# Gelu and silu on two items at once, third-level key sums, earlier x tiles and held-back values in a planned attention + MLP kernel

## Chip, cores, metric

One core of one Trainium2 chip. The metric is device microseconds of a whole execution; smaller is better. ACT is the scalar engine, DVE the vector engine, PE the matmul engine (PEld its weight loads), POOL the GpSimd engine, SP the engine that issues transfers. Spans in a profile are 1.8 to 2.4 us shorter than the time that is reported for the run. "Granted clock" is the share of the full PE clock that the trace shows as granted.

## The reference, cut

```python
xn = layernorm(x)                       # x: 2048 x 1024, bf16
q, k, v = split(xn @ wqkv)              # 32 heads of 32
s = softmax(q k^T / sqrt(32)) v @ wo    # attention
h = gelu(layernorm(xn) @ w1 + b1)       # 3584 wide, tanh form
g = silu(h @ w2 + b2)
return x + s * g
```

## The kernel before

The kernel doesn't write its instruction order by hand. It records operations with estimated durations, runs a list scheduler over them on the host (the *planner*), and emits each engine's instructions in the order that came out. The order is then fixed: an engine that waits for one instruction can't take the next.

Eight groups of four heads give 512 *units* (256 queries x 256 keys x 4 heads). A unit is 8 score matmuls, two exponentials of 1024 columns on ACT, and 8 matmuls with V. Softmax denominators come from matmuls with a matrix of ones ("ones-quads", 4 column-tiled matmuls each). To need fewer of them, DVE first adds key blocks of the exponentials together. Between the units PE does the *dense* work: projections, w1, w2 and, near the end, the output projection wo.

```python
def commit(o, t):                                  # planner: a DMA
    ...
        state["bw"] = max(state["bw"], t) + o.nbytes / 210.0     # bytes per ns
        o.fin = state["bw"] + 1900.0
    ...
def unit(u, pv):                                   # scores, then exponentials
    o = add("PE", s_fn, 235.0, TL, ..., mode="r")  # row tiled
    for h in range(2):
        x = act(... ACT.Exp ..., c_act(1024), ..., 0)
    ...
def ones_pair(u, pv):                              # two units
    pa = dve(PA[a0:a0+2] = P[..,0,:] + P[..,1,:])  # first level, 2048 columns
    pb = dve(PA[a0] = PA[a0] + PA[a1])             # second level, 1024
    ...                                            # late ones are dropped; PE then does more quads
    if u < NOPA or ...: plan.skip.append(pa)       # NOPA = 24: none for the first 24 units
def w1_item(c, pi):                                # 256 x 256 of the hidden layer
    ... 16 matmuls in 8 chunks ...
    dve(xb = psum + b1); dve(sq = xb * xb); dve(ut = (sq + 1/GA) * xb)
    act(ut = tanh(GC * GA * ut))                   # 512 columns
    dve(h = (ut + 1) * xb)
```

The softmax here doesn't subtract the row's maximum and nothing guards it: scores larger than these inputs give would overflow.

## Time and profile before

| | before |
|---|---|
| time, runs of the first comparison | 1062.28 us median (1061.9 to 1063.47, 4 runs) |
| span of the profiled run | 1060.2 us |
| busy PE / DVE / ACT | 97% / 89% / 97% |
| first-level and second-level adds on DVE | 243 and 219 |
| ones-quads on PE | 319 |

The lines are in the prediction below. An ACT record lasts longer than the slot that its instruction takes: exponentials are 1243 ns long on average, but their median distance from start to start is 904 ns. I therefore measure *spacing*, from the start times in the trace, and cut every run in three:

- **start**: start of exponential 32 (counted from 0), by when the prologue is over;
- **middle**: from there to the start of the last exponential, number 1023;
- **tail**: from there to the end of the span.

Within the middle, *excess* is what exponentials are spaced above 904 ns, and a *gap* is a single one over 300 ns. The kernel before has start 63.97, middle 981.06, tail 15.19; 10.83 us of excess, but not one gap. (The recorded expectations below quote starts and tails from another zero; they differ by up to 0.5 us from the ones here, which count from the first instruction as `prof` does.)

### The profile page before, as it was taken

The page shows a single profiled execution, that of the slowest core. Times are in us where ns is not written, and L with a number is a line of the kernel's source. Part 1 is how long each engine was busy: PE and PEld are TensorE (multiplying, and loading weights), DVE is VectorE, ACT ScalarE, POOL GpSimd, SP SyncE. Part 2 cuts the span into 40 slices and gives each one's busy share as a digit, 9 for nine tenths or more (in the row PEclk, how much of TensorE's full clock was granted, in tenths as well). Part 3 has the DMA queues.
Part 4 walks back from the last instruction along what each step waited for, and adds up shares of the span by engine and source line. Part 5 has one row for each costly group of instructions (what it writes and reads, how often), then busy time and mean ns, then how long its engine had stood idle before and what let it go on. Part 6 is the DMA issues. An engine that isn't in the chain of part 4 may idle for free.

```text
span 1060.2 us, 32647 instructions
## 1 busy us (share of the span) xinstructions
PE 1026.5 (97%) x14502; PEld 643.7 (61%) x14562; DVE 946.9 (89%) x1585; ACT 1028.9 (97%) x1186; POOL 31.2 (3%) x42
## 2 busy tenths in 40 slices
PE   7999999999999999999999999999999999999998
PEld 5756466556665566566665566466665666665443
DVE  8479898999999998899989998999999998978996
ACT  4999999999999999999999999999999999999994
POOL 5500000000000000000000000000000000000000
PEclk9999999999999999999999999999999999999999
DMA  9335166522674466423763476224765776662442
GB/s 268 111 96 158 42 179 190 144 76 71 186 207 126 113 193 196 113 57 112 206 192 105 122 199 195 74 76 121 212 180 151 221 217 190 179 197 70 134 140 87
DMA packets 285798, 156.52 MB, mean 148 GB/s; under 512 B 23642, under 2 KB 276570, under 8 KB 285658
## 3 DMA queue, kind: packets, MB, share of 16 engines
q1 hardware_dynamic: 285658, 154.44, 51.0%
q8 instruction: 114, 1.87, 0.8%
q14 instruction: 26, 0.21, 0.1%
HBM read 142.35 MB, written 12.06 MB: 146 GB/s over the span
## 4 chain that ended last, share of the span: by engine, by line
ACT 93%; PE 4%; DVE 2%; DMA 1%; issue 0%; SPq 0%; POOL 0%; POOLq 0%
ACT P L1067 86%; ACT ut L939 5%; PE ps L668 3%; ACT gw L971 2%; DVE stats L823 1%; DMA hT<-in_A_x_dram 1%; PE ps L663 1%; ACT big L814 0%; PE ps L1058 0%; PE ps L803 0%; DVE yT L911 0%; POOL gw L847 0%; DVE V L740 0%; DVE mv L825 0%; SPq L693 0%
## 5 line engine op out<-in xcount | busy, mean ns | idle before, releaser
L1067 ACT ACTIVATE P<-ps 128x1024 bf16<-128x1024 f32 x1024 | 986.8, 1243 | 5.3 <-PE ps L1058 5.3
L1087 DVE TENSOR_TENSOR PA<-P 128x2048 bf16<-128x2048 bf16 x243 | 294.7, 1215 | 25.4 <-ACT P L1067 24.1
L668 PE MATMUL ps<-yT,w1r 128*128 128x256 bf16 x1792 | 234.9, 275 | 2.3 <-DVE xb L931 1.1
L668 PE MATMUL ps<-w2r,hT 128*128 128x256 bf16 x1792 | 226.9, 273 | 0.3 <-DVE nv L1121 0.2
L668 PEld LDWEIGHTS ps<-yT,w1r 128*128 128x128 bf16 x1792 | 162.1, 98 | 60.5 <-issue 28.6
L668 PEld LDWEIGHTS ps<-w2r,hT 128*128 128x128 bf16 x1792 | 162.2, 98 | 51.0 <-issue 30.5
L1091 DVE TENSOR_TENSOR PA<-PA 128x1024 bf16<-128x1024 bf16 x219 | 147.7, 684 | 1.4
L663 PE MATMUL ps<-P,V 128*32 128x256 bf16 x4096 | 142.8, 274 | 0.6 <-DVE xb L931 0.4
L668 PE MATMUL ps<-big,qk 128*128 128x512 bf16 (+2 forms) x522 | 120.9, 357 | 5.7 <-issue 2.1
L668 PE MATMUL ps<-qk,big 128*128 128x256 bf16 (+1 forms) x723 | 121.2, 305 | 2.5 <-issue 1.3
L663 PEld LDWEIGHTS ps<-P,V 128*32 128x32 bf16 x4096 | 97.7, 96 | 33.1 <-issue 19.6
L1058 PE MATMUL ps<-QKT 32*128 32x256 bf16 x2048 | 101.7, 273 | 7.4 <-ACT P L1067 5.9
L1058 PE MATMUL ps<-qk 32*128 32x256 bf16 x2048 | 101.9, 273 | 6.2 <-ACT P L1067 2.1
L939 ACT ACTIVATE ut<-ut 128x512 f32<-128x512 f32 x112 | 94.5, 855 | 0.0
L668 PEld LDWEIGHTS ps<-qk,big 128*128 128x128 bf16 x736 | 65.3, 98 | 41.5 <-issue 13.3
L931 DVE TENSOR_TENSOR xb<-ps,b1T 128x512 bf16<-128x512 f32 x112 | 76.6, 684 | 13.9 <-PE ps L668 12.6
L941 DVE SCALAR_TENSOR_TENSOR hT<-ut,xb 128x512 bf16<-128x512 f32 x112 | 76.4, 684 | 5.9 <-ACT ut L939 5.2
L668 PEld LDWEIGHTS ps<-big,qk 128*128 128x128 bf16 x568 | 47.7, 98 | 52.4 <-issue 15.6
L1058 PEld LDWEIGHTS ps<-QKT 32*128 32x128 bf16 x2048 | 30.3, 92 | 76.6 <-ACT P L1067 75.9
L937 DVE SCALAR_TENSOR_TENSOR ut<-sq,xb 128x512 f32<-128x512 bf16 x112 | 76.1, 682 | 0.3
L1058 PEld LDWEIGHTS ps<-qk 32*128 32x128 bf16 x2048 | 30.4, 92 | 71.6 <-ACT P L1067 67.4
L663 PE MATMUL ps<-PA,ones 128*32 128x256 bf16 x1068 | 56.0, 274 | 0.3 <-DVE PA L1091 0.3
(75 smaller groups left out, 532.2 us busy)
## 6 DMA issues: line engine op xcount, KB each, us to landing
w1r<-in_B_w_dram SPq DMA_DIRECT2D x112, 512.0 KB, 4.4
w2r<-in_B_w_dram SPq DMA_DIRECT2D x128, 448.0 KB, 4.4
qk<-in_A_wqkv_dram SPq DMA_DIRECT2D x16, 256.0 KB, 3.2
g_scratch<-gw SPq DMA_DIRECT2D x32, 128.0 KB, 3.0
o_scratch<-ot SPq DMA_DIRECT2D x56, 64.0 KB, 2.8
big<-o_scratch SPq DMA_DIRECT2D x28, 128.0 KB, 3.5
hT<-in_A_x_dram SPq DMA_DIRECT2D x10, 256.0 KB, 5.5
qk<-in_A_wqkv_dram SPq DMA_DIRECT2D x4, 512.0 KB, 4.4
```

The lines of the kernel that those rows point to most:

```text
L663: ins = e.matmul(dst(j), lhsT=lhsT(j), rhs=rhs(j), start=start, stop=stop, tile_position=(0, 32 * j), skip_group_check=True)
L668: return e.matmul(dst, lhsT=lhsT, rhs=rhs, start=start, stop=stop, skip_group_check=True)
L823: dve(lambda e, t=t, c=c: e.bn_stats(stats[:, t, c, :], xst[t][:, c * 512:(c + 1) * 512]), 600, [XS(t)], [("st", t, c)], 1)
L931: dve(lambda e: e.tensor_tensor(xb_t[i3][:].rearrange("p (k t) -> p k t", k=2), bank(it.bank).rearrange("p (k t) -> p k t", k=2), b1T[:, 2 ...
L937: dve(lambda e: e.scalar_tensor_tensor(ut_t[i3][:], sq_t[p % 2][:], 1.0 / GA, xb_t[i3][:], op0=ALU.add, op1=ALU.mult), c_f32(512), [("sq", ...
L939: act(lambda e: e.activation(ut_t[i3][:], ut_t[i3][:], ACT.Tanh, scale=GC * GA), c_act(512), [("ut", i3)], [("ut", i3)], 1)
L941: dve(lambda e: e.scalar_tensor_tensor(hT[:, hs].rearrange("p k t -> p (k t)"), ut_t[i3][:], 1.0, xb_t[i3][:], op0=ALU.add, op1=ALU.mult), ...
L971: act(lambda e: e.activation(zh_t[zi], z_t[zi], ACT.Tanh, scale=0.5), c_act(512), [("z", zi)], [("zh", zi)], 1)
L1058: ins = e.matmul(bank(b0[j], kk * 256, (kk + 1) * 256), lhsT=QKT[sl][32 * j:32 * j + 32, 1, kb * 128:(kb + 1) * 128], rhs=QKT[sl][32 * j:3 ...
L1067: x = act(lambda e, h=h: e.activation(P[pi][:, 2 * h:2 * h + 2].rearrange("p j k q -> p (j k q)"), ps[:, pr[h] * 1024:(pr[h] + 1) * 1024], ...
L1087: pa = dve(lambda e: e.tensor_tensor(PA_all[:, a0:a0 + 2].rearrange("p u j q -> p (u j) q"), P_all[:, p0:p0 + 2, :, 0, :].rearrange("p u j ...
L1091: pb = dve(lambda e: e.tensor_tensor(PA[a0][:], PA[a0][:], PA[a1][:], op=ALU.add), c_b16(1024), [("PA", a1)], [("PA", a0)], PBPRIO)
```

## The change

Its intent: fewer ACT instructions (one tanh for two items), less PE work (a third level of key sums; value matmuls placed after scores so that PE changes its tiling mode less), an earlier start. The diff, cut to its core:

```diff
-GRACE2 = 600 ; RESERVE = 300 ; NOPA = 24 ; OLAG = 1 ; GRACE1 = 8000
+GRACE2 = 1200; RESERVE = 800 ; NOPA = 0  ; OLAG = 0 ; GRACE1 = 2500
+GRACE3 = 600 ; FINE = 1 ; XF = 3 ; ADJ = 300 ; SPLIT = 2       (further dates changed)
@@ planner
-                state["bw"] = max(state["bw"], t) + o.nbytes / 210.0
+                state["bw"] = max(state["bw"], t) + o.nbytes / 280.0
@@ planner, opening a value item
+                        r = max(bf[0], it.chunks[0].ready, it.trigger.fin)
+                        if state["mode"] != "r" and state["dopen"] is not None:
+                            r = max(r, it.trigger.fin + ADJ)
@@ planner, prologue: work that is due may interrupt an open value item   (cut)
@@ DMA issue on SP
-            return add("SP", fn, 70, ...)
+            return add("SP", fn, 430, ...)
@@ x tiles
-        load_x(0)
-        load_x(1)
+        for t in range(XF):
+            load_x(t)
         wk0 = load_qk(0, 1)
         wq0 = load_qk(0, 0)
@@ w1_item (w2_item's silu likewise)
-            for k in range(8):                      # chunks of two matmuls
+            for k in range(16 // FINE):             # of one
+            if p % 2 == 0:
+                return it
+            dve(h = xb * xb)                        # 1024
+            dve(ut = (h + 1/GA) * xb)               # 1024
+            act(ut = tanh(...))                     # 1024
+            for r in halves: dve(h[r] = (ut[r] + 1) * xb[r])
@@ key sums, now for four units
+            add8 = dve(PA[a0] = PA[a0] + PA[a2])    # third level, 1024
```

Not shown: the planner's other estimates changed too, among them the q and k weight loads, counted at 1.5 times their bytes.

## The prediction

> **What bounds the kernel now.** I read the page first, then ACT's own waits, then the chain in order of time, then the groups by form, and last the two ends as timelines. The page's sums leave three candidates:
>
> ```profile
> PE 1026.5 (97%) x14502; PEld 643.7 (61%) x14562; DVE 946.9 (89%) x1585; ACT 1028.9 (97%) x1186; POOL 31.2 (3%) x42
> ...
> ACT 93%; PE 4%; DVE 2%; DMA 1%; issue 0%; SPq 0%; POOL 0%; POOLq 0%
> ```
>
> PE and ACT both show 97%, but the chain that ended last is 93% ACT. The waits decide it:
>
> ```profile
> PEld ps L1058 <- ACT P L1067: 143.3, 490, 1.3
> ...
> ACT big L814 <- PE ps L803: 11.2, 7, 6.0
> ...
> ACT P L1067 <- PE ps L1058: 5.3, 5, 3.0
> ```
>
> The score matmuls' weight loads (L1058) wait 143.3 us in all for the exponentials (L1067) to free a PSUM pair; ACT waits 16.5 us in the whole run (and 0.7 us at the very start). PE runs ahead of ACT, not behind. ACT's timeline shows where its idle time lies:
>
> ```profile
> 8.19 1.51 ACT L814 ACTIVATE big<-ps 128x1024 bf16<-128x1024 bf16 x2 [5.98 <-PE ps L803]
> 12.69 1.94 ACT L1067 ACTIVATE P<-ps 128x1024 bf16<-128x1024 f32 x2 [2.98 <-PE ps L1058]
> ...
> 20.67 1.94 ACT L814 ACTIVATE big<-ps 128x1024 bf16<-128x1024 bf16 x2 [2.46 <-PE ps L803]
> ...
> 61.63 1.94 ACT L1067 ACTIVATE P<-ps 128x1024 bf16<-128x1024 f32 x2 [0.92 <-PE ps L1058]
> ```
>
> The bracket is idle time before the row. After 61.6 us there is none until the last exponential ends at 1046.1 us (start 1039.47 plus 6.62): 984.46 us of wall time, 984.45 busy. So the time is startup idle 0.7 + 11.2 + 5.3 = 17.2 us, ACT work 1028.9, and a tail of 1060.2 - 1046.1 = 14.1. Sum 1060.2, the span; the timed median is 1.9 us longer.
>
> ACT's work by kind, from the merged chain:
>
> ```profile
> 110.53 26.56 ACT P L1067 x29
> 137.60 9.17 ACT P L1067 x10
> ...
> 621.12 1.01 ACT ut L939 x2
> ```
>
> 26.56 / 29 gives 0.916 us per exponential; the gap from 110.53 + 26.56 = 137.09 to 137.60 is one tanh of 512 columns, 0.51 us. (The group page's 1243 and 855 ns are start-to-end times which overlap; spacing is what counts.) Check: 1024 x 0.9165 + 144 x 0.513 (112 gelu, 32 silu) + 16 transposed copies (14.9) + 1.5 = 938.5 + 73.9 + 14.9 + 1.5 = 1028.8.
>
> **What the Trainium skill says.** "Perfetto Trace Analysis", Identifying the Most-Contended Engine, says matmul occupancy is no measure for TensorE and that occupancy serves for ScalarE. The trace agrees: PE's 97% hides 143 us of load waits, ACT's 97% is real. "VectorE: DVE Perf Modes", The TRN2 errata, says SBUF-source operations of VectorE and ScalarE pay a fixed cost once per instruction, so one larger tile pays it once. ACT agrees: an exponential takes 0.9165 for 1024 columns; if a column costs the page's 1.2 GHz cycle, 0.833 ns, the exponential leaves 0.063 us fixed and the 512-column tanh 0.513 - 0.427 = 0.086. "TensorEngine Tiling (Array Packing)", Key Properties, says that changing tiling mode drains TensorE; that is what putting values (column tiled) next to scores (row tiled) is to save. Here such a drain would lie in PE time that is not on the path.
>
> **The change part by part.**
>
> *Gelu and silu on pairs.* 144 tanh of 512 become 72 of 1024. A tanh of 1024 is estimated at 0.086 + 0.853 = 0.94 us. Saving 72 x (2 x 0.513 - 0.94) = 72 x 0.086 = 6.2 us of ACT, all on the path, since ACT has no idle time there. With the slope of the two PSUM copies instead ((1033 - 592) / 512 = 0.86 ns) it would be 5.2. I take 6.
>
> *DVE side of the pairs.* Square: 112 x 0.416 become 56 x 0.684 (the 1024-column bf16 add of L1091 is the same form), 8.3 us less. The add-and-multiply before tanh: 112 x 0.682 become 56 x 1.22 (0.684 = 0.153 fixed + 1.04 ns x 512, so 1.22 for 1024), 8 us less. Silu's last step, 2.4 us less. The product into hT stays in halves. Together 19 us less DVE, off the path.
>
> *Third-level sums.*
>
> ```profile
> L1087 DVE TENSOR_TENSOR PA<-P 128x2048 bf16<-128x2048 bf16 x243 | 294.7, 1215 | 25.4 <-ACT P L1067 24.1
> L1091 DVE TENSOR_TENSOR PA<-PA 128x1024 bf16<-128x1024 bf16 x219 | 147.7, 684 | 1.4
> L663 PE MATMUL ps<-PA,ones 128*32 128x256 bf16 x1068 | 56.0, 274 | 0.3 <-DVE PA L1091 0.3
> L663 PE MATMUL ps<-P,ones 128*32 128x256 bf16 x208 | 7.1, 273 | 0.0
> ```
>
> Before, 256 pairs of units need (1068 + 208) / 4 = 319 ones-quads. A third add of 0.684 us for each of 127 groups of four would be 87 us of DVE; no longer leaving out the first 24 units adds 12 x 1.215 + 12 x 0.684 = 23; the longer grace of the second level brings back at most the 23 adds dropped as late (256 - 12 - 2 - 219), 16 us. 946.9 + 87 + 23 + 16 - 19 = 1054, which is the whole span, so the planner must drop about half of the third adds as late. I expect 40 to 90 of them and DVE at 94 to 97%. PE then needs about 200 quads; 115 fewer at 0.11 us (spacing of the P,ones quads: 48 matmuls in 1.49 us at 51.4) are 13 us of PE. None of it is on the path but in the tail.
>
> *x tiles ahead of weights.*
>
> ```profile
> 2.72 5.91 DMA hT<-in_A_x_dram
> 8.65 1.29 DVE stats L823 x2
> 10.38 0.56 DVE stats L823
> ```
>
> The third x tile is issued at 2.72 behind the two weight slices and lands at 8.63; DVE has holes until then and is then busy without a break to 34.6, giving statistics for one pair of tiles every 3.5 us. With that tile third in the queue, its two statistics (1.3 us) move into the holes. The fourth tile has the same bytes ahead of it and gains nothing. So all of the key production moves up by about 1.3 us. The weights come later by some 256 KB at 281 GB/s, 0.9 us: with landings of 4.3 to 4.8 us after issues at 1.6 and 2.1 they arrive at about 7 to 8, still ahead of their first use at 9.27. Letting key work interrupt an open value item in the prologue, and planning DMA issue at its true 430 ns, may give another 1 us. The first 9 us of ACT idle (5.98 + 2.98) depend on tiles 0 and 1 and stay. Startup idle 17.2 becomes about 15.
>
> *Tail.* After the last exponential PE has 42 matmuls of 512 columns, 9.24 us in the chain. The last block's four output items need 4 x 8 = 32; the other 10 (2.2 us) are older work that was late. With 13 us of PE freed some of it gets done earlier; I take half, 1.1 us.
>
> *The rest* (new projection dates, single-matmul chunks, holding values back 300 ns, smaller buffers merged, statistics kept in the tanh buffer) moves PE and DVE work about within a loop that ACT bounds: 0, with some risk.
>
> Sum: 1028.9 - 6 = 1022.9 work; 15 + 13 idle; span 1051, time 1052.8. I say 1052.5.
>
> **The rivals.**
>
> *DVE becomes the bound.* For: 89% now, and up to 107 us of adds want in. The chain evacuation, square, add, tanh, product gets longer with pairs (two instructions of 1.2 us instead of 0.7 between PSUM and hT), and ACT runs in a fixed order, so a tanh or a score pair planned too early stalls it. Against: the adds that are late are dropped when planned, evacuations keep first priority, and ACT waits for DVE nowhere in the trace before. It would show as ACT waiting on the ut tile. Cost 5 to 25 us: 1058 to 1078.
>
> *PE was the true bound.* For: 97% busy. Then fewer ones-quads (13 us) and fewer mode drains count in full, and the time would go to 1035 or so. Against: PE's loads wait 143 us on ACT while ACT has no gap for 984 us; ACT's work alone plus the two ends cannot go below 1022.9 + 9 + 11 = 1043 span. I give it 2%.
>
> *The startup gain is hidden anyway.* POOL needs 0.70 + 0.19 + 2 x 1.2 = 3.3 us per pair of tiles against DVE's 3.5, so an earlier tile may only move the wait to POOL, and the weights may arrive late for 9.27. Then 1055.
>
> **Range and chances.** The pairs' 5 to 6 us are nearly sure; startup and tail 0 to 6 more; new waits up to 8 the other way. Range 1046.5 to 1059.5. Faster by 2% needs 1041, below the 1043 + 1.9 that ACT's work allows: 3%. Slower by 2% (above 1083) needs ACT idle of over 25 us in the middle: 3%.
>
> **What would show it.** Right: ACT work 1022 to 1024 us with 72 tanh of 1024 spaced about 0.94, no ACT idle between some 60 us and the last exponential, third tile landing before 7 us and the second pair of exponentials before 21.5 instead of 22.49, fewer than 250 ones-quads, DVE at 94 to 97%, tail 12 to 14 us. Wrong: ACT waits on DVE or on scores in the middle totalling over 3 us, exponentials spaced other than 0.9165, startup idle under 12 or over 18.

## The result, and the profile after

1064.17 us median (1062.75 to 1064.93, 4 runs) against 1062.28. Ratio 1.0014, 95% interval 0.9997 to 1.0032: the same. Ratios here are the mean time of one kernel's fast runs over that of the other's fast runs of the same rounds, so not quite the ratio of the medians quoted. The changed kernel was timed in this first comparison only. In the later rounds the kernel before took 1060.6 to 1060.8, so the difference of a variant to the changed kernel comes out 1 to 3 us lower by the times than by the ratios, which are used below.

The page of the changed kernel, engines and the chain that ended last:

```profile
PE 1025.0 (97%) x14334; PEld 637.7 (60%) x14334; DVE 972.6 (92%) x1506; ACT 1024.8 (97%) x1114; POOL 34.1 (3%) x42
...
PE 48%; ACT 43%; DMA 4%; DVE 3%; POOL 1%; issue 0%; POOLq 0%
```

The bound changed its face. The chain was 93% ACT; now PE has 48% of it and DMA 4%. The waits of the changed kernel (who, for whom, us in total, times, longest):

```profile
PEld ps L1125 <- ACT P L1134: 130.5, 450, 2.7
...
ACT big L860 <- PE ps L849: 11.2, 6, 6.3
ACT P L1134 <- PE ps L1125: 9.8, 11, 2.9
...
PE ps L714 <- DMA w1r<-in_B_w_dram: 4.4, 7, 1.1
```

ACT's wait for scores went from 5.3 to 9.8 us, and PE now waits for w1 weights, which it did not before. The groups by form (count, busy us, mean ns):

```profile
L1155 DVE TENSOR_TENSOR PA<-P 128x2048 bf16<-128x2048 bf16 x251 | 303.9, 1212 | 16.6 <-ACT P L1134 15.4 <-PE ps L714 0.5
...
L1160 DVE TENSOR_TENSOR PA<-PA 128x1024 bf16<-128x1024 bf16 x202 | 137.8, 689 | 1.7
...
L709 PE MATMUL ps<-PA,ones 128*32 128x256 bf16 x968 | 49.3, 276 | 0.1
...
L1163 DVE TENSOR_TENSOR PA<-PA 128x1024 bf16<-128x1024 bf16 x58 | 40.0, 690 | 1.3
...
L709 PE MATMUL ps<-P,ones 128*32 128x256 bf16 x80 | 2.9, 273 | 0.0
```

58 third-level adds survived; second-level ones fell by 17 (202, were 219). Ones-quads are (968 + 80) / 4 = 262, were 319.

Where the 1.3 us between the two profiled spans come from:

| us | before | after | difference |
|---|---|---|---|
| start | 63.97 | 63.10 | -0.9 |
| middle | 981.06 | 982.68 | +1.6 |
| - tanh in it | 74.37 | 68.22 | -6.2 |
| - excess of exponentials | 10.83 | 18.60 | +7.8 |
| tail | 15.19 | 15.78 | +0.6 |

So the pairs gave what they should, and the middle took it back, with 10 gaps over 300 ns that sum to 8.4 us. **The middle.** One gap, in the timeline of the changed kernel (start us, length us, engine, and in brackets the idle time before and its releaser):

```profile
199.24 2.55 SPq L936 DMA_DIRECT2D w1r<-in_B_w_dram  x2
...
204.66 0.38 PE L714 MATMUL ps<-yT,w1r 128*128 128x256 bf16 x2 [1.09 <-DMA w1r<-in_B_w_dram]
...
205.42 1.94 ACT L1134 ACTIVATE P<-ps 128x1024 bf16<-128x1024 f32 x2 [0.75 <-PE ps L1125]
```

Two w1 matmuls stand in PE's order in front of the next scores. Their weights are not there, PE waits 1.09 us, the scores come late, and ACT is idle for 0.75. The weights landed at 204.5, 5.29 us after the issue at 199.24.

By what PE had waited for just before them, the ten gaps divide so: seven (5.4 us of the 8.4) follow a wait for w1 weights, one (0.35) a wait for w2 weights, one (1.57, at 101.73) a stretch at half clock that is shown further down, and one (1.05, at 909.02) a wait for DVE, which had not yet emptied a PSUM bank:

```profile
907.27 1.36 PE L714 MATMUL ps<-yT,w1r 128*128 128x256 bf16 x11 [0.86 <-DVE xb L985]
...
909.02 1.94 ACT L1134 ACTIVATE P<-ps 128x1024 bf16<-128x1024 f32 x2 [0.65 <-PE ps L1125]
```

**The start.** The same view of the changed kernel, from 33.8 us:

```profile
33.84 1.21 DVE L1155 TENSOR_TENSOR PA<-P 128x2048 bf16<-128x2048 bf16 x1
33.88 1.73 POOL L888 TENSOR_TENSOR lnp<-lnp,mhalf 128x2 f32<-128x2 f32 x1
...
35.31 1.21 DVE L1155 TENSOR_TENSOR PA<-P 128x2048 bf16<-128x2048 bf16 x1
...
35.69 0.89 POOL L890 TENSOR_TENSOR lnp<-lnp 128x2 f32<-128x2 f32 x1
...
39.11 1.02 ACT L860 ACTIVATE big<-ps 128x1024 bf16<-128x1024 bf16 x1 [1.66 <-PE ps L849]
```

and the same two POOL operations in the kernel before:

```profile
34.68 0.70 POOL L842 TENSOR_TENSOR lnp<-lnp,mhalf 128x2 f32<-128x2 f32 x1
35.46 0.19 POOL L844 TENSOR_TENSOR lnp<-lnp 128x2 f32<-128x2 f32 x1
```

The exponentials were well ahead at first (number 8 started at 32.74, before at 37.18). Then DVE began key-sum adds, which the kernel before does not do for its first 24 units; POOL's power operation took 1.73 us instead of 0.70 and its small multiply 0.89 instead of 0.19, the last normalised tiles came late, and ACT waited. Number 12 started at 42.75, before at 43.32.

**The tail** is PE work: in the merged chain the changed kernel ends on

```profile
1048.12 10.05 PE ps L714 x46
```

that is 46 output matmuls after the last ones-quads, against 42 before,

```profile
1047.59 9.24 PE ps L668 x42
```

of which 32 belong to the last block and can't come earlier.

### The profile page after: what moved, and what is told of

The parts are those of the page before. It is cut to its first block, busy times and chain, and to the rows that moved or that the text cites. A ratio compares the mean times of both kernels' runs of the same rounds, so it can differ in the third digit from the quotient of the medians.

```text
span 1061.6 us, 32119 instructions
## 1 busy us (share of the span) xinstructions
PE 1025.0 (97%) x14334; PEld 637.7 (60%) x14334; DVE 972.6 (92%) x1506; ACT 1024.8 (97%) x1114; POOL 34.1 (3%) x42
## 4 chain that ended last, share of the span: by engine, by line
PE 48%; ACT 43%; DMA 4%; DVE 3%; POOL 1%; issue 0%; POOLq 0%
ACT P L1134 40%; PE ps L714 32%; PE ps L1125 8%; PE ps L709 8%; DMA w1r<-in_B_w_dram 3%; ACT ut L1000 3%; DVE ut L869 1%; DMA w2r<-in_B_w_dram 1%; POOL gw L898 0%; POOL lnp L912 0%; DMA hT<-in_A_x_dram 0%; DVE xb L985 0%; DVE PA L1155 0%; DVE lnp L884 0%; ACT gw L1036 0%
## 5 line engine op out<-in xcount | busy, mean ns | idle before, releaser
L1134 ACT ACTIVATE P<-ps 128x1024 bf16<-128x1024 f32 x1024 | 960.7, 1189 | 10.2 <-PE ps L1125 9.8
L1155 DVE TENSOR_TENSOR PA<-P 128x2048 bf16<-128x2048 bf16 x251 | 303.9, 1212 | 16.6 <-ACT P L1134 15.4
L709 PE MATMUL ps<-P,V 128*32 128x256 bf16 x4096 | 146.3, 276 | 1.1 <-ACT P L1134 0.5
L1160 DVE TENSOR_TENSOR PA<-PA 128x1024 bf16<-128x1024 bf16 x202 | 137.8, 689 | 1.7
L714 PE MATMUL ps<-big,qk 128*128 128x512 bf16 (+2 forms) x568 | 130.6, 360 | 2.6 <-DVE V L786 0.8
L714 PE MATMUL ps<-qk,big 128*128 128x256 bf16 (+1 forms) x736 | 124.8, 306 | 0.4 <-DVE V L1301 0.2
L1003 DVE SCALAR_TENSOR_TENSOR hT<-ut,xb 128x512 bf16<-128x512 f32 x112 | 74.1, 680 | 2.2 <-ACT ut L1000 2.0
L998 DVE SCALAR_TENSOR_TENSOR ut<-hT,xb 128x1024 f32<-128x1024 bf16 x56 | 68.2, 1220 | 0.1
L1000 ACT ACTIVATE ut<-ut 128x1024 f32<-128x1024 f32 x56 | 67.3, 1207 | 0.0
L1199 DVE STREAM_TRANSPOSE nt<-ps 128x256 f32<-128x256 f32 x64 | 28.7, 449 | 27.5 <-PE ps L709 27.1
```

The costliest lines, as they stand in the source:

```text
L709: ins = e.matmul(dst(j), lhsT=lhsT(j), rhs=rhs(j), start=start, stop=stop, tile_position=(0, 32 * j), skip_group_check=True)
L714: return e.matmul(dst, lhsT=lhsT, rhs=rhs, start=start, stop=stop, skip_group_check=True)
L998: dve(lambda e, r=r: e.scalar_tensor_tensor(ut_t[i2][:, r], h[:, r], 1.0 / GA, xb[:, r], op0=ALU.add, op1=ALU.mult), c_f32(r.stop - r.star ...
L1000: act(lambda e: e.activation(ut_t[i2][:], ut_t[i2][:], ACT.Tanh, scale=GC * GA), c_acts(1024), [("ut", i2, 0), ("ut", i2, 1)], [("ut", i2, ...
L1003: dve(lambda e, r=r: e.scalar_tensor_tensor(h[:, r], ut_t[i2][:, r], 1.0, xb[:, r], op0=ALU.add, op1=ALU.mult), c_f32(r.stop - r.start), [ ...
L1134: x = act(lambda e, h=h: e.activation(P[pi][:, 2 * h:2 * h + 2].rearrange("p j k q -> p (j k q)"), ps[:, pr[h] * 1024:(pr[h] + 1) * 1024], ...
```

## Experiments

Theory 1: the planner's DMA rate, 280 instead of 210, makes it count on weights that have not landed. From the planner's own record and the landings in the trace, 109 w1 loads after 60 us, issue to landing:

| | planned, mean us | measured, mean us | later than planned by over 1 us |
|---|---|---|---|
| before (210) | 4.91 | 4.56 | 4 |
| after (280) | 3.84 | 4.57 | 38 |

Rivals: the longer chain of a pair, or DVE's added load, starves ACT. The edits are against the changed kernel unless the label begins with "before". All ran with five rounds; the kernel before measured 1060.6 to 1060.8 on the chips of these runs.

**The rate alone, put back.**

```diff
-o.nbytes / 280.0
+o.nbytes / 210.0
```

> The changed kernel with one planner constant put back: 210 instead of 280 bytes per ns for DMA. Theory (the planner counts on weights too early, so the fixed PE order puts w1 and w2 matmuls in front of scores before the weights have landed; eleven ACT gaps of over 0.3 us, 8.7 us in all): PE's waits on w1r loads (4.4 us, 7 times) go to under 1 us, ACT's waits on scores after 65 us from 5.1 to under 1.5 us, time 4 to 8 us less than the changed kernel, 1056 to 1060. Rival (the pairs' longer chain through DVE or the third sums' load starve ACT): still 1062 to 1066.

1061.99 us, ratio 1.0008 (0.9996 to 1.0021). The trace has the predicted middle: 975.89 us, 6.8 less than the changed kernel, no ACT wait on scores shown after 67 us, w1 waits gone. The time misses the expectation (1056 to 1060): the whole plan changed with the constant, and the start became 65.85, 2.8 us later. Theory 1 stands for the middle of this plan; the rivals fall as the main cause, since pairs and third sums are all there. DVE keeps its one gap of 1.05 us in the changed kernel.

**The rate alone, in the kernel before.**

```diff
-o.nbytes / 210.0
+o.nbytes / 280.0
```

> The kernel before with that one constant set to 280. Theory: it alone brings ACT gaps of near 1 us at w1 loads, and the time goes up by 4 to 9 us, to 1066 to 1071. Rival (the stalls need pairs or third sums): within 2 us of before.

1070.36 us, ratio 1.0089. The number is inside the expected 1066 to 1071 and the reason is not the expected one: no gap over 300 ns, middle 981.65, though 25 of the 109 loads landed over 1 us late. All of it is tail: 22.10 us, with 75 output matmuls after the last ones-quads. So the rate does not make gaps by itself; what else of the change it needs is open. And there is a second account in which time is lost: dense work that doesn't get done between the units piles up behind them.

**No third-level sums.**

```diff
-(add8, 1, u < NOPA or u + 4 >= last)
+(add8, 1, True)
```

> The changed kernel without any third-level add (58 fewer DVE adds, about 58 ones-quads more on PE). If third sums load DVE so that ACT starves, the time falls by 3 us or more. If PE is short and they help, it rises by 3 us or more. Theory: neither is on the path, within 3 us of the changed kernel; the weight-landing stalls stay.

1068.72 us, ratio 1.0068, 5.7 us above the changed kernel by the ratios (0.0054 x 1061). "PE is short and they help" was right, my own theory wrong. PE has (14566 - 14334) / 4 = 58 quads more, at 0.11 us 6.4 us; the middle hardly moved (982.00) and the tail grew by 5.8, to 21.59:

```profile
1048.48 15.88 PE ps L714 x73
```

(Merged chain of this run.) PE's work, one for one, came out in the tail.

**Tanh split again on ACT.**

```diff
-act(ut[1024] = tanh(...))
+for r in halves: act(ut[r] = tanh(...))
```

> The changed kernel with each gelu tanh of 1024 columns split again into two of 512 on ACT, DVE left as it is. Spacing measured 0.947 against 2 x 0.520 us: 56 x 0.093 = 5.2 us more ACT work. If ACT bounds the loop the time rises by 4 to 6 us, to 1068 to 1070; if PE or the DMA waits bound it, by under 2 us.

1070.08 us, ratio 1.0089, 8 us above the changed kernel by the ratios, 5.9 by the times; expected were 4 to 6. The middle grew by 4.6: tanh takes 5.2 us more in it and the excess fell by 0.5. So ACT work does count in the middle, nearly one for one; start +0.8, tail +0.6 in the profiled run.

**No key sums in the first 24 units.**

```diff
-NOPA = 0
+NOPA = 24
```

> The changed kernel, but the first 24 units get no key-sum adds on DVE, as in the kernel before. Theory (DVE's key-sum adds at 33.8 to 38.9 us slow the POOL operations of the last tiles: power 0.70 to 1.73, small multiply 0.19 to 0.89, so the last copies on ACT wait): no POOL power or normalisation longer than 0.75 and 1.25 us, startup idle of ACT falls by 2 to 4 us, exponential 32 starts at 60 to 61.5 instead of 63.3. The middle keeps its weight stalls, 5 to 10 us in gaps over 0.3 us. Time 2 to 4 us less than the changed kernel. Rival (startup is bound by DVE statistics or PE whatever the adds do): exponential 32 at 63 or later.

1058.39 us, ratio 0.9986 (0.9971 to 1.0001), 3.0 us below the changed kernel by the ratios. Exponential 32 starts at 59.43, 3.7 us earlier than in the changed kernel, and POOL is undisturbed (its timeline in this run):

```profile
33.80 0.70 POOL L888 TENSOR_TENSOR lnp<-lnp,mhalf 128x2 f32<-128x2 f32 x1
34.57 0.19 POOL L890 TENSOR_TENSOR lnp<-lnp 128x2 f32<-128x2 f32 x1
```

A little more than expected: 59.43 against 60 to 61.5. Up to exponential 28 the lead is 2.9 us (55.8 against 58.7); the rest comes where the changed kernel has half clock, from 59.5 to 62.9 us, and this run has none. The middle keeps 9 gaps, 5.7 us.

**The rate put back only after the prologue.**

```diff
-o.nbytes / 280.0
+o.nbytes / (280.0 if t < 60000 else 210.0)
```

> The changed kernel with the planner's DMA rate 280 up to 60 us and 210 after it. Theory: startup as in the changed kernel (exponential 32 at 63 to 64), middle as in the run with 210 throughout (no ACT gap over 0.3 us; exponentials 32 to 1023 in 975 to 977 us against 982.7), time 4 to 7 us below the changed kernel and 3 to 6 below before. Rival (the gain in the middle of that run was chance, of that one plan): gaps come back at other places and the middle is 980 or more.

1060.42 us, ratio 0.9993 (0.9981 to 1.0005), 2.2 us below the changed kernel by the ratios: half of what was expected. Start 63.09 and all but one of the w1 gaps gone (2 of 109 loads later than planned by over 1 us), but the middle is 979.21, not 975 to 977, and has 7 gaps, 4.8 us. As the rival said, gaps came at other places, though its 980 was not reached. Two of them, 2.08 and 0.67 us, lie between 100 and 105 us. The changed kernel has a gap there too (1.57 us at 101.73), which follows something else. Windows of the changed kernel (busy us of PE, PEld, DVE, ACT and POOL with counts, granted clock of PE, DMA):

```profile
93.00:96.00 3.00, 0.72 (x11) 0.16 (x9) 2.97 (x6) 3.00 (x4) 0.00 (x0) 1.00 0.82 239
96.00:99.00 3.00, 2.31 (x48) 1.65 (x52) 2.97 (x4) 3.00 (x4) 0.00 (x0) 0.67 0.26 76
```

PE had almost nothing to do for over 3 us, its mean granted clock was 0.67 in the next window and 0.76 in the one after (it is 0.50 from 97.0 to 100.4 us), and the values that follow took nearly twice their time: 48 matmuls in 2.75 us, where 48 of the same shape in the kernel before took 1.49. In the run with the late rate the clock is 0.50 from 97.0 to 103.8 us. That the empty stretch lowered the clock is read from the order of events; no run tests it.

**Both repairs.**

```diff
+o.nbytes / (280.0 if t < 60000 else 210.0)
+NOPA = 12
```

> Both repairs: 210 after 60 us, and no key-sum adds for the first 12 units. Theory: exponential 32 at 60 to 61.5, middle 975 to 977, tail 15 to 17.5 (the plan leaves 2 us more of PE work after the last scores): 1.0 to 4 us better than the rate alone, 5 to 8 us below before. Rival: the two gains do not add, since PE work not done in the middle returns in the tail.

1057.19 us (1055.66 to 1057.66), ratio 0.9964 (0.9952 to 0.9975): faster than both kernels, by 0.4%, in the profiled run with start 59.57, middle 975.92 with one gap, and tail 18.09. The two repairs add: 3.1 us over the rate alone. Against before it is 3.8 us, not 5 to 8; the profiled run was the fastest of the five, and the only one at a granted clock of 1.000. Its waits of ACT are down to the prologue:

```profile
ACT big L860 <- PE ps L849: 9.2, 5, 6.4
ACT P L1134 <- PE ps L1125: 3.6, 2, 2.9
```

**The pairs alone, in the kernel before.** The pair code and its buffers, nothing else:

```diff
+if p % 2 == 0: return it
+dve(h = xb * xb); dve(ut = ...); act(ut = tanh) ; for r in halves: dve(h[r] = ...)     # 1024
```

> The kernel before with nothing but the gelu and silu pairs and their buffers. If ACT alone bounds the loop: middle 6 to 7 us shorter (974.5), tail as before (15.2), time 6 us less. If PE bounds it as much, the middle is shorter by 6 us but the output projections that no longer fit pile up after the last scores: tail 20 to 22 us, time within 2 us of before. The plan itself leaves 18.8 us of PE work after the last scores against 12.3 before, which speaks for the second.

1063.0 us, ratio 1.0018 (1.0006 to 1.003): the second branch. The middle is 4.0 us shorter (977.02; a gap of 1.4 us at 100 us took some, after half clock from 96.3 to 99.7), the tail 6.5 longer, 21.70:

```profile
1043.19 15.88 PE ps L671 x73
```

ACT's gain by itself is worth nothing in this plan. The units run faster, the dense work fits less well between them, and four output items more come out behind.

**Values held back longer, with both repairs.**

```diff
-ADJ = 300
+ADJ = 450
```

> Both repairs (210 after 60 us, no key-sum adds for the first 12 units) and values held back 450 ns instead of 300. The plan of the two repairs left 15.1 us of PE work after the last scores, this one 12.9, as in the changed kernel. Theory (the tail is PE backlog, set by the plan): exponential 32 at 59.6 to 60, middle 975 to 977, tail 15.4 to 16 instead of 17.9; time 1.5 to 3 us below the two repairs, 5 to 7 us below before. Rival (tail set by the output transfers and normalisation): tail stays near 17.9.

1056.2 us, ratio 0.9958 (0.9946 to 0.9971), the best time of all, but only 0.6 us below the two repairs and their intervals overlap. The tail is 15.76, 2.3 shorter, as expected from the plan. The middle is 979.61, 3.7 us longer than that of the two repairs, with 4.6 us in gaps; 3.3 of them, at 98 us and from 903 to 906, follow stretches at half clock (94.1 to 97.5 and 899.6 to 903.1). The profiled run was the slowest of the five.

**Values not held back.**

```diff
-ADJ = 300
+ADJ = 0
```

> The changed kernel with values not held back at all (0 instead of 300 ns). The plan then has 1190 changes of tiling mode on PE instead of 1176 and leaves 18.6 us of PE work after the last scores instead of 12.9. Theory: start and middle as in the changed kernel within 2 us, tail 21 to 22 us instead of 15.6, time 5 to 7 us above the changed kernel. Rival (PE has slack, mode changes cost nothing): within 2 us of the changed kernel.

1069.74 us, ratio 1.0072, 6.2 us above the changed kernel by the ratios. Middle 983.26, tail 21.53: it is the backlog again. Holding values until scores have gone saves 14 changes of tiling mode in the plan (1176 against 1190). Whether it is these or another arrangement that the 300 ns bring along, this run can't tell.

**Two x tiles ahead instead of three**, without key sums in the first 24 units:

```diff
+NOPA = 24
-XF = 3
+XF = 2
```

> The changed kernel without key-sum adds in the first 24 units (its ACT start is then 59.58 us for exponential 32) and with two x tiles ahead of the weights as before, not three. Theory (the third tile early moves 1.3 us of statistics into DVE's holes): exponential 32 at 60.5 to 61.5, time 1 to 2 us above the same kernel with three. Rival (POOL at 3.3 us a pair paces the startup, so a tile more ahead is hidden): exponential 32 within 0.4 us of 59.58.

1057.69 us, ratio 0.9965 (0.9953 to 0.9978), where 1 to 2 us above the kernel with three (0.9986) were expected; the intervals overlap, and at a granted clock of 1.000 both take 1056.2 to 1057.8. Exponential 32 at 60.12, 0.7 later: between the theory (0.9 to 1.9) and the rival (at most 0.4). The second pair of tiles is 1.2 us earlier on ACT with three tiles (exponential at 20.51 against 21.68), and 0.5 of it is lost again in the rest of the prologue. So the third tile's 0.7 us of start is not seen in the time.

All runs, from one profiled execution each (us), with that execution's mean granted clock; time and ratio are of all executions:

| run | clock | start | middle | gaps: number, us | tail | matmuls in tail | time | ratio |
|---|---|---|---|---|---|---|---|---|
| before | 0.998 | 63.97 | 981.06 | 0 | 15.19 | 42 | 1062.28 | 1 |
| after | 0.997 | 63.10 | 982.68 | 10, 8.4 | 15.78 | 46 | 1064.17 | 1.0014 |
| after_bw210 | 0.998 | 65.85 | 975.89 | 2, 0.8 | 15.79 | 46 | 1061.99 | 1.0008 |
| before_bw280 | 1.000 | 62.73 | 981.65 | 0 | 22.10 | 75 | 1070.36 | 1.0089 |
| after_no8 | 0.995 | 64.15 | 982.00 | 6, 4.7 | 21.59 | 73 | 1068.72 | 1.0068 |
| after_split | 0.992 | 63.95 | 987.31 | 8, 7.5 | 16.34 | 49 | 1070.08 | 1.0089 |
| after_nopa24 | 1.000 | 59.43 | 979.70 | 9, 5.7 | 15.79 | 46 | 1058.39 | 0.9986 |
| after_late210 | 0.995 | 63.09 | 979.21 | 7, 4.8 | 15.79 | 46 | 1060.42 | 0.9993 |
| after_late210_nopa12 | 1.000 | 59.57 | 975.92 | 1, 0.5 | 18.09 | 57 | 1057.19 | 0.9964 |
| before_pairs | 0.997 | 63.75 | 977.02 | 1, 1.4 | 21.70 | 73 | 1063.0 | 1.0018 |
| best_adj450 | 0.994 | 60.34 | 979.61 | 6, 4.6 | 15.76 | 46 | 1056.2 | 0.9958 |
| after_adj0 | 0.994 | 64.05 | 983.26 | 10, 6.6 | 21.53 | 73 | 1069.74 | 1.0072 |
| after_nopa24_xf2 | 1.000 | 60.12 | 979.48 | 7, 5.1 | 15.79 | 46 | 1057.69 | 0.9965 |

The changed kernel and its variants scatter by 1 to 6 us from run to run; the kernel before by about 1.5. Much of that goes with the granted clock. Without key sums in the first 24 units, the three runs at 1.000 took 1057.3 to 1057.6, the two at 0.998 1059.2 and 1059.6, and the one at 0.997 1063.1. So a segment can be off by 1 to 2 us for a stretch at half clock that another execution doesn't have, and the times decide.

One number was on the host before any run. The expectations give, for five of the plans, the PE work left after the last scores: 12.3 (before), 12.9 (changed kernel), 15.1 (both repairs), 18.8 (pairs alone) and 18.6 us (values not held back). Their tails are 15.19, 15.78, 18.09, 21.70 and 21.53: the planned backlog plus 2.9 to 3.0 us each time.

## Why the prediction was wrong, point by point

- **The pairs' saving of 6 us of ACT: right in size.** 74.37 - 68.22 = 6.2 us; a tanh of 1024 is spaced 0.947 us, estimated 0.94. (The 0.9165 per exponential, by contrast, already held 12 ns of excess on average; the median is 0.904. And the exponential reads PSUM, so it is no test of what the cited page says of SBUF sources. The tanh is one: 2 x 0.520 us against 0.947.) What was wrong is "all on the path, since ACT has no idle time there". In the kernel before, the pairs alone gave 4 us in the middle and cost 6.5 in the tail.
- **"The rest [...] moves PE and DVE work about within a loop that ACT bounds: 0, with some risk." This is the term that failed.** It measured +7.8 us of excess between exponentials, and the prediction's own sign of being wrong, ACT waiting for scores for over 3 us in the middle, came true with 5 us. Most of it is PE, in its fixed order, waiting for w1 weights in front of the scores. I passed over the planner's constants, above all the DMA rate, as bookkeeping. With a fixed order they decide what stands in front of the scores. Putting the rate back removed 6.8 us of the middle in one plan, and 3.5 to 3.8 in two others (979.21 against 982.68; 975.92 against 979.70, where NOPA differs too). Of the 4.8 us of gaps that stayed in the first of these, 2.75 follow PE at half clock after an empty stretch.
- **Startup "17.2 becomes about 15": the early part was right, the sum was not.** The third tile's statistics began at 5.97 us and the second pair of exponentials at 20.57, before 21.5 as said; but the idle time of ACT up to exponential 32 was 16.8 us. I priced "no longer leaving out the first 24 units" as 23 us of DVE time off the path. It lay across POOL's path instead, and cost 2.9 to 3.7 us of start. The Trainium skill has this: "SBUF — State Buffer", Who interferes with whom, says that a DVE instruction with two SBUF inputs contends with a GpSimd instruction that reads SBUF. I had not looked there. The trace agrees: 0.70 us grew by 1.03 beside an add of 1.21. The rival that POOL hides the startup gain came nearest to what happened, though it was DVE's adds that held POOL up and not the earlier tile.
- **Tail 14.1 becomes 13: wrong.** From the end of the last exponential to the end of the span it became 14.6, and PE had 46 matmuls left, not fewer than 42.
- **Third-level sums:** 58 adds, inside 40 to 90. But 262 quads were left, not "about 200" or "fewer than 250", and DVE is at 92%, not 94 to 97%, because the second level did not come back: 202 of its 256 adds ran, where the prediction's terms counted on 254. One is left out by rule, and 53 were late. "None of it is on the path but in the tail" was right, and I took the tail for 1.1 us: without the sums it is 5.8 us longer.
- **The rival that PE bounds, given 2%:** half right. PE waits 130 to 143 us for ACT in all and is short nevertheless. What it can't do between the units is done after the last one. Three different edits (no third sums, values not held back, pairs alone) each moved the tail by some 6 us.
- **The rival that DVE starves ACT:** nearly absent. ACT itself waits for DVE nowhere in the changed kernel, but one of the ten gaps, 1.05 us at 909.02, came through PE, which had waited 0.86 us for DVE to empty a bank.

So the change's parts are of 4 to 6 us each, and they do not add: what the pairs save in the middle shortens the time only if third sums and held-back values keep the dense work out of the tail, and then a planner constant and a collision with POOL took back as much. Open: what the 280 needs besides itself to make gaps, as the kernel before did not get them, and what decides in which executions PE drops to half clock.

## What to carry to other kernels

In a kernel that is scheduled ahead, treat each constant of the model as part of the change: compare planned with measured landings, and the planned backlog of each engine at the end, before looking at any engine. Late landings alone need not make gaps: the kernel before, with the rate at 280, had 25 and not one gap. Read a bound loop in three parts, start, steady part and tail; time saved on the engine that bounds the steady part returns in the tail when another engine's backlog is just as full. And before work is put into a "free" engine, look at what reads SBUF beside it at that moment.

## What the Trainium skill lacked or had wrong

- "Perfetto Trace Analysis", Identifying the Most-Contended Engine: occupancy is called a fair measure for ScalarE. Here ACT's records overlap (1243 ns long, 904 apart), so 100% busy hid 10.8 us of excess in the kernel before (1% of the span; 6.5 us of it in 61 spacings of over 50 ns), and 18.6 in the changed kernel. Start-to-start spacing shows it.
- "TensorE: Matmul & The Clock Gate", Part 1: it ties the lower clock to an idle window of about 3.4 us. Here two idle stretches of 0.59 and 2.38 us, with 8 score matmuls between them, were followed by 3.4 us at a granted clock of 0.50.
- No page: that in a kernel with a fixed order a DMA rate assumed a third higher goes with 3.5 to 6.8 us more in the middle of the changed kernel, although landings differ from the plan by only 0.7 us on average (3.84 planned, 4.57 measured), and with next to nothing in the middle of the kernel before (981.65 against 981.06).
